# An attention kernel's turns: six score tiles set aside instead of five, P.V sums copied by ScalarE

## The chip, the cores and the metric

The kernel runs on one core of a Trainium2 chip. The metric is the device time of one execution in microseconds (us). All data are 32-bit floats; matmuls of linear layers and scores take operands of the type fp32r, and where more precision is needed an operand is split into a high and a low part and three products are added (high x high, high x low, low x high).

## What is computed

With x of 2048 rows by 512, 32 heads of 16, and a feed-forward part with 1792 hidden columns:

```python
q, k, v = split_heads(layernorm(x) @ wqkv)
p = softmax(einsum("bhqd,bhkd->bhqk", q, k) * 16 ** -0.5)
s = merge_heads(einsum("bhqk,bhkd->bhqd", p, v)) @ wo
h = relu(layernorm(x) @ w1 + b1) ** 2          # einsums in the reference
out = x + s * silu(h @ w2 + b2)
```

(In the reference the feed-forward part takes the same normed x.)

## The kernel before, in words

After a preparation of some 135 us (norms, transposes, q, k and v) comes the main part, the loop `for n in range(TURNS)` at the end of `fast_path`: 64 turns. A turn handles eight steps of attention; a step is one block of 128 keys against 512 queries for four heads. Two turns make up the 16 key blocks of one group of four heads (`qd`) and one chunk of 512 queries (`qc`). The order of instructions on every engine is written out by hand: no scheduler moves anything, and an instruction waits on semaphores for what it needs.

**Scores.** A step has two score pairs. A pair is two matmuls over 64 rows each (one in either half of TensorE's rows, side by side), which write the transposed scores of two heads, 128 keys by 2 x 512. A *direct* pair goes to one of two rotating PSUM buffers S of two banks each (`scores`), and ScalarE takes its exp from there into a tile P in SBUF (`exps`, line 519, form P<-S, 128x1024). A pair *set aside* (`aside`) goes half by half into two single banks, `sides[0]` = acc and `sides[1]` = lin; VectorE copies each half to the tile P (line 538), and ScalarE takes the exp later, from SBUF to SBUF (form P<-P).

**The linear work of a turn.** Beside the scores a turn runs a pair of blocks of the feed-forward layers or of the output projection (`Block`, `lin`), two outputs of 128x512, each of 12 products that are cut into two halves of 64 rows. Each block owns one bank of the tile `spare`. Half way, at the *row swap* (`swap`), the blocks change row halves; since two row halves may not write one bank at a time, GpSimd sets a one-element tile (`note`, line 588) when the products so far are done, and the first product after the swap waits for that: the fence.

**The row string.** The order of a turn on TensorE is a string. One letter is one *slot*, two matmuls over 64 rows side by side: S is a direct score pair, L a half of either block, B both halves of a pair set aside, 0 or 1 one half of such a pair (into acc or lin) beside one half of a block, / the swap, which is no slot. An ordinary turn's string has 40 slots, numbered 0 to 39 here:

```python
ORDINARY = "SLLSBLLLSLL0SL1LSLL/SBLLSLL0SL1LSLL0L1SLS"
```

TWO_PAIRS, SHORT and FIRST are the strings of turns 2, 16, 30 and 44, of turns 56 and 57, and of turn 0. Of a turn's 16 score pairs the first nine and the last two are direct, five are set aside. ScalarE's queue holds the exps in the order: the first nine, the five, the last two, which belong to the next turn's first step.

**P.V and what follows.** After its 40 slots a turn multiplies the P tiles of eight steps by V (`values_of`, line 866): 64 records of 128 rows by 32 columns, summed in the bank acc. Then `finish(n)`: after an even turn VectorE copies the sum to a tile `ou` (line 889), after an odd one it adds acc to that (line 892), and SP stores the result with five DMAs (`zd`, four `ud`), behind which the row sums are loaded again (`zc`, line 910), to be read by VectorE at the end of the next turn's slots (lines 903 to 915). At the start of each turn `see` (lines 1129 and 1130) lets ScalarE and VectorE touch the last tile set aside in the turn before.

VectorE and GpSimd also split weights and hidden values into parts (`split_piece`, `evict` in `first`): VectorE casts, GpSimd subtracts (line 120). `pieces_of` gives each turn 0, 1 or 2 such weight pieces; a second, late one falls to turns 6 and 10 of every 14. `middle` holds the turns (13, 14, 27, 28, 41, 42, 58, 59) with an extra tanh on ScalarE.

Of the kernel before, what the change touches and what calls it, by code (L numbers as in the profile page):

```python
# [28 lines left out]
OP = mybir.AluOpType  # L29
# [47 lines left out]
def fast_path(tc, sb, banks, env):  # L77
# [7 lines left out]
    dve, act, pool, sp = nc.vector, nc.scalar, nc.gpsimd, nc.sync  # L85
# [6 lines left out]
    def t(shape, dt, tag):  # L92

        cnt[0] += 1
        if tag in BUFS:
            turn[tag] = turn.get(tag, -1) + 1
            n = turn[tag] % BUFS[tag]
            p, tag = ps.get(tag), f"{tag}{places[n] if tag == 'S' else n}"
        else:
            p = None  # L100
        return (p or ps.get(tag, sb)).tile(shape, dt, tag=tag, name=f"{tag}_{cnt[0]}")
# [10 lines left out]
    def cast(eng, dst, src):  # L112
        if eng is act:
            act.copy(dst, src)
        else:
            eng.tensor_copy(dst, src)  # L116
# [392 lines left out]
    ptile = {}  # L509

    def score(i, p, hp, dst):
        qd, qc, kb = steps[i]
        k, q = ka[qd, kb // 8], qa[qd, qc]
        r = slice(64 * hp, 64 * hp + 64)
        mm(dst, k[r, p, 128 * (kb % 8):128 * (kb % 8) + 128], q[r, p], start=True, stop=True)  # L515

    def exps(i, p, src):
        if src is not None:
            act.activation(ptile[i, p], src, AF.Exp, scale=SCALE)  # L519

    def place(i, p):
        ptile[i, p] = t([128, 2, 512], FT, f"P{2 * ((i - 1) % 8) + p}")

    def scores(i, p):

        if i < len(steps):
            sc = t([128, 2, 512], FT, "S")
            place(i, p)
            for hp in range(2):
                score(i, p, hp, sc[:, hp])  # L530
            return sc

    def aside(i, p, hp):

        if hp == 0:
            place(i, p)
        score(i, p, hp, sides[hp])
        dve.tensor_copy(ptile[i, p][:, hp], sides[hp])  # L538
# [37 lines left out]
    def lin(*halves):  # L576
        done = False
        if pair[0]:
            for half in halves:
                j = half ^ swapped[0]  # L580
                done |= pair[0][j].issue(half, lin_banks[j])
        return done
# [11 lines left out]
    def end_pair():  # L594
        if pair[0]:
            while lin(0, 1):
                pass
            swapped[0], last, pair[0] = 0, pair[0], None
            last[0].evict()
# [46 lines left out]
    def second(c, g, i):  # L646
        ms = [m for m in range(len(PAIRS)) if PAIRS[m][0] == g]
        h, w = [hid[m] for m in ms], [wf[2, m] for m in ms]

        def evict():  # L650
            if g == 0:
                y[c, i] = t([128, 2, 512], FT, f"y{i}")
            old = b2b.unsqueeze(1).broadcast_to([128, 2, 512]) if g == 0 else y[c, i]
            dve.tensor_tensor(y[c, i], spare, old, op=OP.add)
            if g == 3:
                complete.add((c, i))

        return [Block(lambda p, k, j=j: h[k // 2][p][:, k % 2, 128 * j:128 * j + 128],
                      lambda p, k: w[k // 2][p][:, k % 2], range(2 * len(ms)), evict)
                for j in (2 * i, 2 * i + 1)]  # L660
# [8 lines left out]
    fill = []  # L669
    for c in ORDER:  # L670
        for m in range(len(PAIRS)):
            fill.append([lambda m=m: first(m)])
            if m in (1, 2, 4, 6):
                makes = [lambda c=c, g=m // 2, i=i: second(c, g, i) for i in range(2)]
# [188 lines left out]
    def values(i, first, last):  # L863
        qd, qc, kb = steps[i]
        for j in (1, 2, 3, 0) if i % 2 else (0, 1, 2, 3):
            mm(sides[0][32 * j:32 * j + 32], vq[qd][:, kb, 17 * j:17 * j + 32], ptile[i, j // 2][:, j % 2],  # L866
               start=first, stop=last)

    part, early = [None], [None]

    def values_of(steps_now):
        for i in steps_now:
            values(i, i == steps_now[0], i == steps_now[-1])

    def finish_early():
        early[0] = t([128, 512], FT, "ou")
        dve.tensor_copy(early[0], sides[0])

    def finish(n):

        if n == TURNS - 1:
            return
        if early[0]:
            part[0], early[0] = early[0], None
            dve.tensor_tensor(part[0], sides[0], part[0], op=OP.add)
            return
        ou = t([128, 512], FT, "ou")
        if n % 2 == 0:
            dve.tensor_copy(ou, sides[0])
            part[0] = ou  # L890
            return
        dve.tensor_tensor(ou, sides[0], part[0], op=OP.add)  # L892
        qd, qc, _ = steps[8 * n]
        sp.dma_start(zdram[qd][qc], ou[16::32])
        for j in range(4):
            sp.dma_start(udram[qd // 2][qc][0, qd % 2, :, j], ou[32 * j:32 * j + 16])
        events.setdefault(2 * n + 2, []).insert(0, (load_rowsums, (qd, qc)))
        events.setdefault(2 * n + 3, []).insert(0, (rowsums, (qd, qc)))
# [140 lines left out]
    middle = {}  # L1039
    TURNS, LAST = len(steps) // 8, 8 * (NQ - 1)  # L1040
# [8 lines left out]
    for j, c in enumerate(ORDER):  # L1049
        for i in range(2):  # L1050
            n = per * (j + 1) + i - 1 if j < 3 else LAST + 2 + i
# [41 lines left out]
    def happen(time):  # L1093
        for fn, a in events.pop(int(2 * time), ()):
            fn(*a)
# [6 lines left out]
    sides = [t([128, 512], FT, "acc"), t([128, 512], FT, "lin")]  # L1102
# [23 lines left out]
    def see(i):  # L1126

        last = ptile[i, 1][:1, 1, 511:]
        act.copy(seen[:, :1], last)
        dve.tensor_tensor(seen[:, 8:9], last, sides[1][:1, :1], op=OP.max)  # L1130
# [4 lines left out]
    ORDINARY = "SLLSBLLLSLL0SL1LSLL/SBLLSLL0SL1LSLL0L1SLS"  # L1135
    TWO_PAIRS = "SLSLBLLSL/SBLLSLL0S1LSEVLLSLLB/SSLL0L1S"

    SHORT = "SLLSBLLLS0S1LL0S1/S0LL1SL0SL1L0LSS1"

    FIRST = "SLLSLLBLSLL0SL1LSLL/SBLLSLL0SL1LSLL0L1SLS"  # L1140
    for n in range(TURNS):
        i = 8 * n
        happen(n)
        makes = fill[n][:]
        pair[0] = makes.pop(0)()
        if n:
            see(i - 1)
        pairs = [(k, p) for k in range(i + 1, i + 9) for p in range(2)]
        short = n in (LAST, LAST + 1)
        nd = 8 if short else 9  # L1150
        direct, asides = pairs[:nd] + pairs[14:], pairs[nd:14]
        later, aside_at = [], [0, 0]
        for row in TWO_PAIRS if makes else SHORT if short else ORDINARY if n else FIRST:
            if row == "S":
                k, p = direct.pop(0)
                sc = scores(k, p)
                if k == i + 8:
                    later.append((k, p, sc))
                else:
                    exps(k, p, sc)  # L1160
            elif row == "L":
                lin(0, 1)
            elif row in "01B":
                for hp in (0, 1) if row == "B" else (int(row),):
                    aside(*asides[aside_at[hp]], hp)
                    aside_at[hp] += 1
                if row != "B":
                    lin(1 - int(row))
            elif row == "/":
                swap()  # L1170
                if n == TURNS - 1:
                    make_last()
            elif row == "E":
                end_pair()
                pair[0] = makes.pop(0)()
            else:
                values_of(range(i, i + 2))
                finish_early()
        for j, (k, p) in enumerate(asides):
            exps(k, p, ptile[k, p])  # L1180
            if j == 0:
                for fn, a in middle.pop(n, ()):
                    fn(*a)
        for a in later:
            exps(*a)
        if n == TURNS - 1:
            two = t([128, 2, 512], FT, "S")
            for m in range(2):
                rest(m, two[:, m])
            rest(3, sides[1])  # L1190
        pieces_now = pieces_of[n] if n < len(pieces_of) else 0
        ahead = pieces_now > 0 and n % per in (0, 1, 3, 6, 7, 10, 11)
        while lin(0, 1):
            pass
        if ahead:
            split_piece()
        end_pair()
        if n == LAST + 4:
            gsb.update({(1, i): y[1, i] for i in range(2)})
        if n == TURNS - 1:  # L1200
            for m in range(2):
                end_rest(m, two[:, m])
            end_rest(3, sides[1])
        happen(n + 0.5)
        for _ in range(pieces_now - ahead):
            split_piece()
        values_of(range(i + 2 if early[0] else i, i + 8))
        finish(n)
    for time in sorted(events):
        happen(time / 2)  # L1210
# [7 lines left out]
    ou = t([128, 512], FT, "P0")  # L1218
# [158 lines left out]
```

## Time and profile before

| | |
|---|---|
| time, median of 3 runs (lowest to highest) | 1209.07 us (1208.68 to 1209.79) |
| profiled execution: its span, the only time of it that the page gives | 1207.8 us |
| what the median has above that span | 1.27 us |
| PE, DVE, ACT, POOL busy in the span | 1198.8, 843.3, 1042.3, 357.3 us |
| one ordinary turn (turn 24) | 533.50 to 549.97 us of the span |

The page names the engines PE (TensorE's matmuls), PEld (its weight loads), DVE (VectorE), ACT (ScalarE), POOL (GpSimd) and SP (SyncE, which issues most DMAs). L515 is line 515 of the kernel. A timeline row has the start, the time from the first start to the last end of the instructions merged in it, engine, line, operation, the names out<-in and the sizes, the number of instructions, and in brackets the idle time before them with what ended it. In matmul rows S<-QA,KA is a direct score pair, acc<-QA,KA or lin<-QA,KA a half set aside, S with other inputs a product of a block, and acc<-P,V is P.V. A group's row ends with busy time, mean ns of one, idle time before them and its releasers.

### The profile page before, as it was taken

The page shows a single profiled execution, that of the slowest core. Times are in us where ns is not written, and L with a number is a line of the kernel's source. Part 1 is how long each engine was busy: PE and PEld are TensorE (multiplying, and loading weights), DVE is VectorE, ACT ScalarE, POOL GpSimd, SP SyncE. Part 2 cuts the span into 40 slices and gives each one's busy share as a digit, 9 for nine tenths or more (in the row PEclk, how much of TensorE's full clock was granted, in tenths as well). Part 3 has the DMA queues.
Part 4 walks back from the last instruction along what each step waited for, and adds up shares of the span by engine and source line. Part 5 has one row for each costly group of instructions (what it writes and reads, how often), then busy time and mean ns, then how long its engine had stood idle before and what let it go on. Part 6 is the DMA issues. An engine that isn't in the chain of part 4 may idle for free.

```text
span 1207.8 us, 24222 instructions
## 1 busy us (share of the span) xinstructions
PE 1198.8 (99%) x9867; PEld 706.4 (58%) x9867; DVE 843.3 (70%) x1362; ACT 1042.3 (86%) x1232; POOL 357.3 (30%) x276
## 2 busy tenths in 40 slices
PE   9999999999999999999999999999999999999997
PEld 7888655555555555555555555555555555555554
DVE  6666767575867766757677666677775758777766
ACT  6655689889999899889999999889899889899984
POOL 5756523040312321304032122220230403322224
PEclk9999999999999999999999999999999999999999
DMA  7798914131353222224323223151422233455534
GB/s 291 292 377 319 333 58 137 45 110 45 97 154 108 72 67 84 72 79 149 119 77 100 60 88 95 45 169 43 133 80 80 78 100 80 132 188 172 160 109 141
DMA packets 107640, 155.17 MB, mean 128 GB/s; under 512 B 43386, under 2 KB 57736, under 8 KB 107524
## 3 DMA queue, kind: packets, MB, share of 16 engines
q1 hardware_dynamic: 104596, 144.60, 37.3%
q0 software_dynamic: 2352, 7.93, 2.1%
q8 instruction: 78, 1.28, 0.4%
q10 hardware_dynamic: 576, 1.05, 0.2%
q14 instruction: 38, 0.31, 0.1%
HBM read 103.87 MB, written 49.67 MB: 127 GB/s over the span
## 4 chain that ended last, share of the span: by engine, by line
PE 99%; DVE 0%; issue 0%; POOL 0%; ACT 0%; POOLq 0%; DVEq 0%
PE acc L866 37%; PE S L563 29%; PE S L515 15%; PE B L326 5%; PE acc L515 5%; PE B L127 4%; PE lin L515 2%; PE D L326 1%; PE D L253 1%; PE B L689 1%; PE S L1017 0%; PE lin L326 0%; PE acc L326 0%; DVE P L1261 0%; DVE P L1262 0%; PE S L326 0%
## 5 line engine op out<-in xcount | busy, mean ns | idle before, releaser
L519 ACT ACTIVATE P<-S 128x1024 f32<-128x1024 f32 x702 | 662.4, 1042 | 92.3 <-PE S L515 90.4
L866 PE MATMUL acc<-P,V 128*32 128x512 f32 x4096 | 453.5, 594 | 0.0
L538 DVE COPY P<-acc 128x512 f32<-128x512 f32 x322 | 222.7, 692 | 140.8 <-PE lin L515 67.9
L519 ACT ACTIVATE P<-P 128x1024 f32<-128x1024 f32 x322 | 315.4, 1092 | 0.0
L866 PEld LDWEIGHTS acc<-P,V 128*32 128x32 f32 x4096 | 126.2, 110 | 285.2 <-issue 265.6
L515 PE MATMUL S<-QA,KA 64*128 64x512 f32 x1404 | 290.4, 404 | 0.0
L538 DVE COPY P<-lin 128x512 f32<-128x512 f32 x322 | 220.5, 685 | 1.5 <-PE lin L515 0.6
L515 PEld LDWEIGHTS S<-QA,KA 64*128 64x128 f32 x1404 | 133.7, 183 | 112.8 <-issue 41.8
L515 PE MATMUL lin<-QA,KA 64*128 64x512 f32 x322 | 126.7, 393 | 0.0
L515 PE MATMUL acc<-QA,KA 64*128 64x512 f32 x322 | 126.4, 392 | 0.0
L120 POOL TENSOR_TENSOR wf1l<-wr,wf1h 128x1024 fp32r<-128x1024 f32 x28 | 68.5, 2446 | 176.9 <-DVE wf1h L116 108.4
L588 POOL MEMSET note<- 1x1 f32 x68 | 6.1, 89 | 381.6 <-PE S L563 381.6
L120 POOL TENSOR_TENSOR hl<-T,hh 128x1024 fp32r<-128x1024 f32 x28 | 80.0, 2858 | 52.9 <-DVE hh L116 52.9
L563 PE MATMUL S<-xl,wf1h 64*128 64x512 f32 x464 | 95.5, 389 | 0.0
L120 POOL TENSOR_TENSOR wf2l<-wr,wf2h 128x1024 fp32r<-128x1024 f32 x28 | 67.3, 2402 | 90.5 <-DVE wf2h L116 90.5
L563 PE MATMUL S<-xh,wf1l 64*128 64x512 f32 x480 | 90.9, 388 | 0.0
L563 PE MATMUL S<-wf2l,hh 64*128 64x512 f32 x448 | 90.1, 389 | 0.0
L892 DVE TENSOR_TENSOR ou<-acc,ou 128x512 f32<-128x512 f32 x31 | 21.4, 692 | 96.6 <-PE acc L866 88.9
L563 PE MATMUL S<-wf2h,hl 64*128 64x512 f32 x448 | 82.6, 388 | 0.0
L563 PE MATMUL S<-xh,wf1h 64*128 64x512 f32 x480 | 77.5, 391 | 0.0
L563 PE MATMUL S<-wf2h,hh 64*128 64x512 f32 x448 | 71.8, 393 | 0.0
L515 PEld LDWEIGHTS acc<-QA,KA 64*128 64x128 f32 x322 | 59.3, 184 | 16.9 <-DVE P L538 2.1
(379 smaller groups left out, 1431.0 us busy)
## 6 DMA issues: line engine op xcount, KB each, us to landing
wr<-in_B_w_dram SPq DMA_DIRECT2D x56, 512.0 KB
QA<-qd SPq DMA_DIRECT2D x128, 128.0 KB
KA<-kd SPq DMA_DIRECT2D x64, 256.0 KB
u<-ud SPq DMA_DIRECT2D x15, 512.0 KB
kd<-P SPq DMA_DIRECT2D x11, 512.0 KB
V<-vd SPq DMA_DIRECT2D x8, 664.0 KB
qd<-P SPq DMA_DIRECT2D x9, 512.0 KB
vd<-P SPq DMA_DIRECT2D x16, 280.0 KB
```

The source lines that it names most:

```text
L120: leng.tensor_tensor(lo, src, hi.bitcast(FT), op=OP.subtract)
L127: mm(dst, lhs(a, k), rhs(b, k), start=n == 0, stop=n == len(todo) - 1)
L253: nc.tensor.transpose(halves[k // 2][:, k % 2, 128 * j:128 * j + 128], xnorm[c, i][:, j, 128 * k:128 * k + 128], ident)
L326: mm(dst, left[a][:, k], right[b][:, k], start=n == 0, stop=n == 5)
L515: mm(dst, k[r, p, 128 * (kb % 8):128 * (kb % 8) + 128], q[r, p], start=True, stop=True)
L519: act.activation(ptile[i, p], src, AF.Exp, scale=SCALE)
L538: dve.tensor_copy(ptile[i, p][:, hp], sides[hp])
L563: ins = mm(bank, self.lhs(a, k)[r], self.rhs(b, k)[r], start=n == 0 and self.at[other] == 0, stop=n == len(self.todo[half]) - 1 and self.a ...
L588: f = pool.memset(note[:, notes[0]:notes[0] + 1], 0.0)
L689: ins = mm(idle[:, :128], ident, ident, start=True, stop=True)
L866: mm(sides[0][32 * j:32 * j + 32], vq[qd][:, kb, 17 * j:17 * j + 32], ptile[i, j // 2][:, j % 2], start=first, stop=last)
L892: dve.tensor_tensor(ou, sides[0], part[0], op=OP.add)
```

## The change

45 of the 64 turns change (1, 3 to 12, 17 to 26, 31 to 40, 45 to 55, 61 to 63): those for which `six(n)` holds, that is neither the first, nor one with TWO_PAIRS or SHORT, nor one in or just behind `middle`. In them

- six of the 16 score pairs are set aside, eight and two are direct, in the order of a new string SIX, again of 40 slots. It has no B; the halves of a pair set aside come in separate slots, which alternate between lin and acc, and two S stand ahead of the swap instead of one S and one B behind it;
- `see` comes at the end of the turn before, ahead of that turn's `finish`, in place of at the start;
- the P.V sum of the turn before is copied out of acc by ScalarE (24 times the plain copy after an even turn, 21 times the copy after an odd turn), and after an odd turn GpSimd adds the earlier sum, both operands in SBUF. The stores then wait for GpSimd.

`place` is called by whichever half of a pair comes first, and `middle` is read without being emptied.

```diff
-        if hp == 0:
+        if (i, p) not in ptile:
             place(i, p)
...
+    def six(n):
+        return 0 < n < TURNS and n not in (LAST, LAST + 1) and len(fill[n]) == 1 and n not in middle and n - 1 not in middle
...
-            dve.tensor_copy(ou, sides[0])
+            cast(act if six(n + 1) else dve, ou, sides[0])
             part[0] = ou
             return
-        dve.tensor_tensor(ou, sides[0], part[0], op=OP.add)
+        if six(n + 1):
+            act.copy(ou, sides[0])
+            pool.tensor_tensor(ou, ou, part[0], op=OP.add)
+        else:
+            dve.tensor_tensor(ou, sides[0], part[0], op=OP.add)
...
+    SIX = "S1SL0LL1SL0LSLLL0L1SS/L0LL1LS0LLS1L0SLL1S"
...
-        if n:
+        if n and not six(n):
             see(i - 1)
...
-        nd = 8 if short else 9
+        nd = 8 if short or six(n) else 9
...
+        if six(n + 1):
+            see(i + 7)
         finish(n)
```

TensorE around the swap of turn 24, before. S with QA,KA is a direct pair, acc and lin are halves set aside, S_278 is the tile of the two blocks; xh_701,wf1l are the last products before the swap, xh_700,wf1h the first behind it:

```order
L563 MATMUL S_278_1650<-xh_701_3914,wf1l_1083_6026 128x512 x4
L515 MATMUL S_1128_6310<-QA_1081_6020,KA_948_5302 128x512 x2
L515 MATMUL acc_1651<-QA_1081_6020,KA_948_5302 128x512
L515 MATMUL lin_1652<-QA_1081_6020,KA_948_5302 128x512
L563 MATMUL S_278_1650<-xh_700_3913,wf1h_1082_6025 128x512 x4
L515 MATMUL S_1131_6324<-QA_1081_6020,KA_948_5302 128x512 x2
```

The same place after the change:

```order
L515 MATMUL lin_1652<-QA_1064_6045,KA_935_5323 128x512
L563 MATMUL S_278_1650<-xh_691_3928,wf1l_1066_6051 128x512
L515 MATMUL S_1109_6336<-QA_1064_6045,KA_935_5323 128x512 x2
L515 MATMUL S_1111_6341<-QA_1064_6045,KA_935_5323 128x512 x2
L563 MATMUL S_278_1650<-xh_690_3927,wf1h_1065_6050 128x512 x2
L515 MATMUL acc_1651<-QA_1064_6045,KA_935_5323 128x512
```

Between the last product before the swap and the first behind it stood a direct pair and a pair set aside; now two direct pairs stand there, and the last product shares its slot with a half set aside.

ScalarE where turn 23 (odd) passes into turn 24, before (P<-S is a direct exp, P<-P one of a tile set aside):

```order
L519 ACTIVATE P_1109_6180<-P_1109_6180 128x1024
L519 ACTIVATE P_1111_6190<-S_1110_6189 128x1024
L519 ACTIVATE P_1113_6196<-S_1112_6195 128x1024
L1129 COPY seen_1653<-P_1109_6180 1x1
L519 ACTIVATE P_1117_6251<-S_1116_6250 128x1024
L519 ACTIVATE P_1119_6260<-S_1118_6259 128x1024
```

The same place after the change:

```order
L519 ACTIVATE P_1091_6205<-P_1091_6205 128x1024
L519 ACTIVATE P_1093_6210<-S_1092_6209 128x1024
L519 ACTIVATE P_1095_6221<-S_1094_6220 128x1024
L1136 COPY seen_1653<-P_1091_6205 1x1
L896 COPY ou_1096_6267<-acc_1651 128x512
L519 ACTIVATE P_1099_6278<-S_1098_6277 128x1024
L519 ACTIVATE P_1102_6287<-S_1101_6286 128x1024
```

The copy of acc, which needs turn 23's last P.V product, now stands ahead of turn 24's first exp.

VectorE from the end of turn 23's work to the first copies of turn 24, before:

```order
L654 TENSOR_TENSOR y_871_4874<-S_278_1650,y_871_4874 128x1024
L892 TENSOR_TENSOR ou_1114_6239<-acc_1651,ou_1085_6063 128x512
L1130 TENSOR_TENSOR seen_1653<-P_1109_6180,lin_1652 1x1
L538 COPY P_1120_6264<-acc_1651 128x512
L538 COPY P_1120_6264<-lin_1652 128x512
L538 COPY P_1123_6284<-acc_1651 128x512
L538 COPY P_1123_6284<-lin_1652 128x512
```

The same place after the change:

```order
L654 TENSOR_TENSOR y_860_4890<-S_278_1650,y_860_4890 128x1024
L1137 TENSOR_TENSOR seen_1653<-P_1091_6205,lin_1652 1x1
L538 COPY P_1100_6282<-lin_1652 128x512
L538 COPY P_1100_6282<-acc_1651 128x512
L538 COPY P_1103_6300<-lin_1652 128x512
L538 COPY P_1103_6300<-acc_1651 128x512
L538 COPY P_1108_6327<-acc_1651 128x512
L538 COPY P_1108_6327<-lin_1652 128x512
```

The addition from acc is gone from VectorE's queue, and the copies of the halves begin with lin.

More of the change, by code (lines that the diff above doesn't have):

```diff
@@ L1149, in fast_path @@
         short = n in (LAST, LAST + 1)
-        nd = 8 if short else 9
+        nd = 8 if short or six(n) else 9
         direct, asides = pairs[:nd] + pairs[14:], pairs[nd:14]
         later, aside_at = [], [0, 0]
-        for row in TWO_PAIRS if makes else SHORT if short else ORDINARY if n else FIRST:
+        for row in TWO_PAIRS if makes else SHORT if short else SIX if six(n) else ORDINARY if n else FIRST:
             if row == "S":
@@ L1181, in fast_path @@
             if j == 0:
-                for fn, a in middle.pop(n, ()):
+                for fn, a in middle.get(n, ()):
                     fn(*a)
```

## The prediction

> **What bounds the kernel now.** I read the page first: its busy table and its chain.
>
> ```profile
> span 1207.8 us, 24222 instructions
> ...
> PE 1198.8 (99%) x9867; PEld 706.4 (58%) x9867; DVE 843.3 (70%) x1362; ACT 1042.3 (86%) x1232; POOL 357.3 (30%) x276
> ...
> PE 99%; DVE 0%; issue 0%; POOL 0%; ACT 0%; POOLq 0%; DVEq 0%
> ```
>
> TensorE (PE) carries the end, but ends of matmuls are modelled, so a busy share of 99% can still hide short waits. I therefore went to the table of stretches for one turn (turn 24; columns: length, then busy time of PE, PEld, DVE, ACT, POOL) and to TensorE's timeline of it.
>
> ```profile
> 533.50:549.97 16.47, 16.47 (x150) 9.18 (x146) 13.48 (x21) 14.95 (x17) 4.17 (x3) 1.00 0.17 43
> ```
>
> ```profile
> 533.50 0.50 PE L515 MATMUL S<-QA,KA 64*128 64x512 f32 x2
> 533.84 0.62 PE L563 MATMUL S<-xh,wf1h 64*128 64x512 f32 x4
> ...
> 535.68 0.85 PE L563 MATMUL S<-xl,wf1h 64*128 64x512 f32 x5
> ...
> 537.50 0.63 PE L563 MATMUL S<-xh,wf1l 64*128 64x512 f32 x4
> 537.96 0.44 PE L515 MATMUL S<-QA,KA 64*128 64x512 f32 x2
> 538.23 0.39 PE L515 MATMUL acc<-QA,KA 64*128 64x512 f32 x1
> ...
> 538.47 0.63 PE L563 MATMUL S<-xh,wf1h 64*128 64x512 f32 x4
> ...
> 539.62 0.39 PE L515 MATMUL acc<-QA,KA 64*128 64x512 f32 x1
> ...
> 542.63 0.40 PE L515 MATMUL S<-QA,KA 64*128 64x512 f32 x2
> 542.96 7.07 PE L866 MATMUL acc<-P,V 128*32 128x512 f32 x64
> 549.97 0.50 PE L515 MATMUL S<-QA,KA 64*128 64x512 f32 x2
> ```
>
> Starts count here, not lengths. P.V takes 549.97 - 542.96 = 7.01 us. Before it stand the 40 slots of the turn's row string: slot 0 takes 0.34, slots 1 to 18 take 537.96 - 533.84 = 4.12 (0.229 each), slot 19, the first after the swap, 0.27, slot 20 0.24, slots 21 to 38 542.63 - 538.47 = 4.16 (0.231 each), slot 39 0.33; together 9.46. The best stretch, slots 9 to 18 from 535.68, runs at 0.228. So no order of the same 40 slots could win more than 9.46 - (0.34 + 38 x 0.228 + 0.33) = 0.13 us a turn; the two end slots stand where matmuls over 64 rows change to P.V's over 128, which no string avoids.
>
> What spoils slots is in the timeline of the weight loads (PEld; in brackets the idle time before, and what ended it):
>
> ```profile
> 537.89 0.19 PEld L515 LDWEIGHTS S<-QA,KA 64*128 64x128 f32 x2 [0.19 <-ACT P L519]
> ...
> 538.35 0.31 PEld L563 LDWEIGHTS S<-xh,wf1h 64*128 64x128 f32 x4 [0.15 <-POOL note L588]
> 538.81 0.18 PEld L515 LDWEIGHTS S<-QA,KA 64*128 64x128 f32 x2 [0.15 <-ACT P L519]
> ...
> 539.40 0.18 PEld L515 LDWEIGHTS acc<-QA,KA 64*128 64x128 f32 x1
> ...
> 542.48 0.19 PEld L515 LDWEIGHTS S<-QA,KA 64*128 64x128 f32 x2
> ```
>
> Around the swap three loads come late: a score pair waits for ScalarE's exp to free its bank, the swapped linear matmul for GpSimd's fence, then another pair for ScalarE. A load 0.12 ahead of its matmul is early enough (538.35 to 538.47), so the second and third cost nothing at once; the first cost slot 19 its extra 0.04. But after such a run the slots stay at 0.231, while slots 9 to 18, with none late, settled at 0.228. I read the one as the cause of the other; the trace shows the order, no more.
>
> **The change part by part.** *TensorE.* 40 slots and 64 P.V records again: nothing added.
>
> *The swap.* The last linear pair before it starts one slot after 537.50, at 537.73; the first after it starts at 538.47, 0.74 later, its load 0.62 later.
>
> ```profile
> 538.21 0.09 POOL L588 MEMSET note<- 1x1 f32 x1 [16.38 <-PE S L563]
> ```
>
> That 0.62 is the matmul's end, this memset and the way back, so the fence lets the first swapped matmul start 0.62 + 0.12 = 0.74 after the last unswapped one. The new string also has two slots between them (S S for S B). If ScalarE no longer delays the first, three slots would take 3 x 0.229 = 0.69, and the fence holds the rest back: the exp's 0.04 is replaced by 0.05 of fence. Ends: -0.05 if the fence comes sooner, +0.02; I take 0.
>
> *The score pairs after it.* Exps follow each other on ScalarE as its timeline shows, and the groups give the length of one (and of a copy, for later):
>
> ```profile
> 534.04 8.39 ACT L519 ACTIVATE P<-S 128x1024 f32<-128x1024 f32 x9 [1.52 <-PE S L515]
> 542.26 4.88 ACT L519 ACTIVATE P<-P 128x1024 f32<-128x1024 f32 x5
> ```
>
> ```profile
> L519 ACT ACTIVATE P<-S 128x1024 f32<-128x1024 f32 x702 | 662.4, 1042 | 92.3 <-PE S L515 90.4
> ...
> L114 ACT COPY P<-B 128x512 f32<-128x512 f32 x14 | 8.1, 586 | 7.0 <-PE B L127 7.0
> ```
>
> One lasts 1.04, the next starts (8.39 - 1.04) / 8 = 0.92 later (0.95 for the five set aside). In the new string pairs stand at slots 0, 2, 8, 12, 19, 20, 27, 31, 35, 39; a pair needs the bank of the pair two before. Counted from the turn's start, slot 19 starts at 0.34 + 18 x 0.229 = 4.46, its exp 0.43 later (as VectorE's copy does, below) at 4.89, slot 20's at 5.81; slots 27, 31, 35, 39 start near 6.3, 7.3, 8.2, 9.1 and need banks whose exps end near 5.9, 6.9, 7.8, 8.7. With 0.05 to the load and 0.12 to the matmul, each has 0.2 or more to spare. So the late loads after the swap go, except the fence's. Slots 21 to 38 should then look like slots 1 to 18: 4.12 for 4.16, and slot 39, whose load at 542.48 was late as well, perhaps 0.01 less: -0.05 a turn. Ends: 0, and 17 x 0.003 + 0.02 = -0.07.
>
> *ScalarE.* One exp goes from PSUM to SBUF (+0.03) and a copy of 128x512 joins: 14.95 + 0.03 + 0.59 = 15.6 of 16.47, so it does not become the bound. The copy waits for P.V's end with next turn's exps behind it. If it starts where VectorE's did, 0.14 into the turn (533.64, below), the first exp starts at 0.73 at the latest, now 0.54. It then ends at 1.77; slot 8 (1.94) wants its load by 1.82, and gets it. The copy's pitch is likely under 0.5, as an exp's is 0.12 under its length, which leaves 0.1. Cost 0; without that cover, 0.1 a turn. At the turn's other end: slot 31's exp starts near 7.7, then 0.92 + 6 x 0.95 + 2 x 0.92 brings ScalarE to 16.2, before it must copy at 16.6.
>
> *VectorE.* Twelve bank copies for ten, P.V's copy or addition gone.
>
> ```profile
> 533.64 0.69 DVE L892 TENSOR_TENSOR ou<-acc,ou 128x512 f32<-128x512 f32 x1 [5.71 <-PE acc L866]
> ...
> 538.66 0.69 DVE L538 COPY P<-acc 128x512 f32<-128x512 f32 x1 [0.72 <-PE lin L515]
> 539.27 0.68 DVE L538 COPY P<-lin 128x512 f32<-128x512 f32 x1
> ```
>
> A bank's round: matmul 538.23, copy 538.66, its end 539.35, next load 539.40, plus 0.12: 1.29, against 6 x 0.229 = 1.37. The new string spaces acc at slots 4, 10, 16, 22, 28, 34 and lin at 1, 7, 18, 25, 32, 38: six or more. Copies follow at 0.61 (538.66 to 539.27), alternation asks for one in three slots, 0.69. Only slots 18 and 34 come two slots after the other bank's; their copies start 0.15 late, but the next use of the bank is seven slots off or is P.V (about 0.1 left). Cost 0. What five slots cost stands in turn 56, where acc is used at 1062.69 and five slots on:
>
> ```profile
> 1062.69 0.39 PE L515 MATMUL acc<-QA,KA 64*128 64x512 f32 x1
> ...
> 1063.87 0.49 PE L515 MATMUL acc<-QA,KA 64*128 64x512 f32 x1
> ...
> 1064.20 0.49 PE L515 MATMUL S<-QA,KA 64*128 64x512 f32 x2
> ```
>
> That slot takes 0.33: 0.10 a miss.
>
> *GpSimd and the queues.* 21 turns get an addition of 128x512, priced by the group of that size; below it are GpSimd's timeline in turn 25, VectorE's there, and SP's in turn 24.
>
> ```profile
> L120 POOL TENSOR_TENSOR P<-P,P 128x512 fp32r<-128x512 f32 x7 | 9.0, 1302 | 5.1 <-ACT P L114 5.1
> ```
>
> ```profile
> 551.66 2.40 POOL L120 TENSOR_TENSOR wf2l<-wr,wf2h 128x1024 fp32r<-128x1024 f32 x1
> 554.67 0.09 POOL L588 MEMSET note<- 1x1 f32 x1 [0.61 <-PE S L563]
> ```
>
> ```profile
> 552.03 0.68 DVE L538 COPY P<-lin 128x512 f32<-128x512 f32 x1
> ```
>
> ```profile
> 534.36 0.54 SPq L894 DMA_DIRECT2D zd<-ou  x1
> ...
> 536.87 0.36 SPq L910 DMA_DIRECT2D zc<-zd  x1
> ```
>
> The addition runs from about 0.8 to 2.1 of the turn, ahead of the fence, due at 538.21 - 533.50 = 4.7; the late splits (wf2l above, done 0.61 before its fence) follow even turns, which have no addition. So 0. Cover gone, a late memset would cost its lateness, in 21 turns. The five stores on SP's queue (from 534.36) and, behind them, the load of the row sums (536.87) and whatever SP issues next move by 1.3; the sums are read after slot 39, past 542.96, four microseconds on: 0.
>
> VectorE's copies beside a GpSimd operation keep their length (0.68 at 552.03, with wf2l running to 554.06), so I add nothing for the new overlap. The Trainium skill (SBUF — State Buffer, Who interferes with whom) says that VectorE and GpSimd share a port pair as an exclusive lock, which a copy takes in its two-port modes; by that rule the addition would hold copies up, which is the rival D below. The trace bears out its exception for an instruction with at most one SBUF input.
>
> *Sum.* -0.05 x 45 = -2.25 us: the profiled span of 1207.8 becomes 1205.5. The shown runs' median, 1209.07, lies 1.27 above that span, so the forecast is 1206.8, its own range 1205.2 to 1208.4. About 0.2% (2.4 us) is what a measurement of this kernel can tell from no change: the forecast is at that edge.
>
> **The rivals.** *A: nothing gained.* If slots at 0.231 don't come from late loads, or if the alternating banks' loads, 0.02 to 0.04 late at six slots, unsettle them as well, the fence replaces the exp's wait and 1209.1 +- 1.5 stays. For it: a mean of 0.229 against 0.231 is little to build on. Against it: slots 9 to 18.
>
> *B: more.* If the fence comes early too, all 0.13 a turn go, 5.9 us: 1203.2. Against it: its 0.62 is the same chain in both orders.
>
> *C: slower, VectorE's banks.* The rounds have 0.08 to spare. If something (a second semaphore to wait for, two slots between the banks) makes a copy start over 0.08 later than I have it, each use misses by about 0.1 as in turn 56: one miss a turn gives 45 x 0.1 = 4.5, 1213.6; all of acc's five, 22, 1231. For it: margins thinner than any now in an ordinary turn. Against it: acc goes six slots now (538.23 to 539.62, its load at 539.40) without a wait.
>
> *D: slower, held copies.* If GpSimd's addition blocks copies, one held for 1.3 makes a score wait up to 1.2, in 21 turns: 25 us, 1234. Against it: 552.03. The same place holds the milder case, ScalarE's copy slower than 0.59: 0.1 x 45, 1213.6.
>
> **How the numbers follow.** Forecast 0.60, A 0.20, B 0.06, C 0.08, D 0.06. The forecast's range lies about half on each side of 1206.65, 0.2% below the median: faster 0.30 + 0.06 = 0.36, same 0.30 + 0.20 = 0.50, slower 0.14. The range leaves out B, C and D, 0.20: it reaches from 1204.9 to A's upper end and a little beyond, 1211.0.
>
> **What would show it.** In a changed turn: slot 19 near 0.23 with no load ended by ScalarE, the fence's load late and slot 20 near 0.28, slots 21 to 38 near 4.12, period 16.42; ScalarE ending before P.V. Wrong would be: loads at slots 10, 16, 22, 28, 34 ended by VectorE (C), late loads at slots 2 or 8 ended by ScalarE, copies over 0.75 beside the addition (D), or slots after the swap still at 0.231 with no load late (A).

## The result, and the profile after

| | before | after |
|---|---|---|
| time, median of 17 runs each (lowest to highest) | 1209.19 us (1208.42 to 1209.83) | 1211.36 us (1210.78 to 1211.98) |
| ratio, 95% interval | | 1.0019 (1.0012 to 1.0025) |
| span of the profiled execution | 1207.8 us | 1209.1 us |

The change costs 2.2 us. The forecast was 1206.8, its range 1204.9 to 1211.0: the result lies 0.36 above it, on the other side of no change. The page of the changed kernel (span, busy row, chain of the end):

```profile
span 1209.1 us, 24425 instructions
...
PE 1200.2 (99%) x9867; PEld 718.2 (59%) x9867; DVE 884.0 (73%) x1411; ACT 1072.9 (89%) x1273; POOL 384.0 (32%) x297
...
PE 98%; DVE 1%; DMA 0%; issue 0%; ACT 0%; DVEq 0%
```

TensorE still carries the end, with the same 9867 matmuls. VectorE, ScalarE and GpSimd have the work that was added and none has become the bound. (ScalarE copies 41 sums, not 45: behind the turns 2, 16, 30 and 44, which have TWO_PAIRS, VectorE still adds the sum, so the changed turns 3, 17, 31 and 45 have no copy on ScalarE.) So most of the loss is to be looked for inside TensorE's stream. One changed turn shows it (turn 20, the start of which is at 467.84; columns of the first fence as in the prediction: length, then PE, PEld, DVE, ACT, POOL):

```profile
467.84:484.32 16.48, 16.48 (x148) 9.60 (x145) 14.26 (x22) 15.67 (x18) 5.21 (x4) 1.00 0.17 43
```

TensorE's timeline of that turn, matmuls:

```profile
467.84 0.50 PE L515 MATMUL S<-QA,KA 64*128 64x512 f32 x2
468.18 0.39 PE L515 MATMUL lin<-QA,KA 64*128 64x512 f32 x1
...
470.03 0.62 PE L563 MATMUL S<-xl,wf1h 64*128 64x512 f32 x3
470.28 0.39 PE L515 MATMUL acc<-QA,KA 64*128 64x512 f32 x1
...
471.17 0.85 PE L563 MATMUL S<-xh,wf1l 64*128 64x512 f32 x5
471.65 0.39 PE L515 MATMUL acc<-QA,KA 64*128 64x512 f32 x1
...
472.33 0.62 PE L515 MATMUL S<-QA,KA 64*128 64x512 f32 x4
472.79 0.44 PE L563 MATMUL S<-xh,wf1h 64*128 64x512 f32 x2
473.06 0.39 PE L515 MATMUL acc<-QA,KA 64*128 64x512 f32 x1
...
476.99 0.40 PE L515 MATMUL S<-QA,KA 64*128 64x512 f32 x2
477.32 1.49 PE L866 MATMUL acc<-P,V 128*32 128x512 f32 x12
```

Slots 1 to 18 take 472.33 - 468.18 = 4.15 (before, in turn 24: 4.12), slots 19 and 20 0.46 together (0.27 + 0.24 before), slot 21 0.27, slots 22 to 38 3.93, slot 39 0.33. The exp's wait at the swap is gone and the fence's is there in its place, as forecast. But the turn is not shorter. Slots 9 to 13 run at (471.17 - 470.03) / 5 = 0.228; from slot 14 on, the next five take (472.33 - 471.17) / 5 = 0.232. The weight loads and VectorE's copies at that place:

```profile
470.07 0.18 PEld L515 LDWEIGHTS acc<-QA,KA 64*128 64x128 f32 x1
...
471.46 0.18 PEld L515 LDWEIGHTS acc<-QA,KA 64*128 64x128 f32 x1
...
472.10 0.42 PEld L515 LDWEIGHTS S<-QA,KA 64*128 64x128 f32 x4
472.73 0.19 PEld L563 LDWEIGHTS S<-xh,wf1h 64*128 64x128 f32 x2 [0.21 <-POOL note L588]
```

```profile
468.61 0.69 DVE L538 COPY P<-lin 128x512 f32<-128x512 f32 x1 [2.62 <-PE lin L515]
469.32 0.69 DVE L538 COPY P<-acc 128x512 f32<-128x512 f32 x1
...
470.71 0.69 DVE L538 COPY P<-acc 128x512 f32<-128x512 f32 x1
```

The load for acc at slot 16 (471.46) comes 0.06 after VectorE's copy of the use before has ended (470.71 + 0.69 = 471.40), and it had to wait for that: the matmuls of the slot before had already begun at 471.39, where most loads begin at once. It still comes 0.19 ahead of its own matmul (471.65), so it delays nothing that a row shows as a wait. Yet here the faster slots end. Before, in turn 24, acc was used at slots 4 and 11, seven slots apart. VectorE's copy of the first use and the load for the second:

```profile
534.96 0.69 DVE L538 COPY P<-acc 128x512 f32<-128x512 f32 x1 [0.57 <-PE lin L515]
```

```profile
535.92 0.18 PEld L515 LDWEIGHTS acc<-QA,KA 64*128 64x128 f32 x1
```

That copy had ended 0.27 ahead of the load, and the load came together with the matmuls of the slot before it. The changed kernel's swap itself (472.10) shows four loads of score pairs and no wait for ScalarE.

Such slots can be counted. For every changed turn ahead of the last (44 turns) I took the difference between the starts of consecutive slots, and the lateness of a load as its start less the start of the matmuls of the slot before. Slots fall in two groups: 0.225 to 0.228, mean 0.2267, called settled here, and the rest, mean 0.232. Means over the same 44 turns:

| us a turn | slot 0 | 1 to 18 | 19 to 21 | 22 to 38 | 39 | sum | settled, 1 to 18 | settled, 22 to 38 |
|---|---|---|---|---|---|---|---|---|
| before | 0.337 | 4.125 | 0.741 | 3.919 | 0.330 | 9.453 | 57% | 33% |
| after | 0.337 | 4.153 | 0.746 | 3.916 | 0.337 | 9.489 | 28% | 32% |

The sums differ by 0.037: 44 x 0.037 = 1.6 us. The last turn is 0.20 longer, the unchanged turns right behind changed ones 0.19 together, the other turns 0.05 shorter: +1.95 from the start of turn 1 to the end of the last turn. The rest of the measured 2.2 lies outside the span: a run of the changed kernel takes 2.04 us more than its own span in the mean, runs of the kernel before 1.77 to 1.80 (those beside the experiments, which list both). Of the experiments' kernels below, the three with the engine part have 2.02 to 2.05 and the others 1.77 to 1.79. So the engine part costs about 0.26 us that no row of a trace shows; why is open. (That the two spans differ by 1.3 only is the preparation and the tail, 0.6 shorter in this execution.)

The same counting tells what ends a settled run. I took the slots behind two settled ones, and the load that starts during such a slot, for the next one. Before (here over all its 54 turns with the ordinary string and 40 full slots), where that load was at most 10 ns later than the one before it, 481 of 482 slots were settled too; where it was later than that, 66 of 98 were. In the 44 changed turns the numbers are 153 of 178 and 32 of 74. So of the 67 ends there 42 come with a late load and 25 without one: the 10 ns are no sharp border. The late ones are halves set aside: median lateness 30, 24, 34, 20, 29 and 33 ns at slots 4, 10, 16, 28, 34 and 38, against 6 to 20 at the others from slot 2 on, but for slots 21 and 22 at the fence. That is rival A's mechanism, so far only read, not shown.

### The profile page after: what moved, and what is told of

Same layout as the page of the kernel before. It is cut to its first block, busy times and chain, and to the rows that moved or that the text cites. A ratio compares the mean times of both kernels' runs of the same rounds, so it can differ in the third digit from the quotient of the medians.

```text
span 1209.1 us, 24425 instructions
## 1 busy us (share of the span) xinstructions
PE 1200.2 (99%) x9867; PEld 718.2 (59%) x9867; DVE 884.0 (73%) x1411; ACT 1072.9 (89%) x1273; POOL 384.0 (32%) x297
## 4 chain that ended last, share of the span: by engine, by line
PE 98%; DVE 1%; DMA 0%; issue 0%; ACT 0%; DVEq 0%
PE acc L866 37%; PE S L563 29%; PE S L515 14%; PE acc L515 5%; PE B L326 5%; PE B L127 4%; PE lin L515 2%; PE D L326 1%; PE D L253 1%; PE S L1024 0%; PE lin L326 0%; PE acc L326 0%; DMA P<-in_A_x_dram 0%; DVE P L1272 0%; DVE P L1273 0%; PE S L326 0%
## 5 line engine op out<-in xcount | busy, mean ns | idle before, releaser
L519 ACT ACTIVATE P<-S 128x1024 f32<-128x1024 f32 x657 | 626.0, 1032 | 49.1 <-PE S L515 47.2
L519 ACT ACTIVATE P<-P 128x1024 f32<-128x1024 f32 x367 | 355.5, 1055 | 0.0
L538 DVE COPY P<-lin 128x512 f32<-128x512 f32 x367 | 252.6, 688 | 104.2 <-PE lin L515 99.1
L538 DVE COPY P<-acc 128x512 f32<-128x512 f32 x367 | 253.4, 690 | 77.5 <-PE acc L515 48.1
L515 PE MATMUL S<-QA,KA 64*128 64x512 f32 x1314 | 264.8, 404 | 0.0
L515 PE MATMUL lin<-QA,KA 64*128 64x512 f32 x367 | 144.2, 393 | 0.0
L515 PE MATMUL acc<-QA,KA 64*128 64x512 f32 x367 | 144.1, 393 | 0.0
L563 PE MATMUL S<-xh,wf1h 64*128 64x512 f32 x480 | 85.1, 395 | 0.0
L515 PEld LDWEIGHTS acc<-QA,KA 64*128 64x128 f32 x367 | 67.4, 184 | 19.3 <-DVE P L538 2.1
L515 PEld LDWEIGHTS lin<-QA,KA 64*128 64x128 f32 x367 | 67.5, 184 | 8.3 <-DVE P L538 0.9
```

The costliest lines, as they stand in the source:

```text
L563: ins = mm(bank, self.lhs(a, k)[r], self.rhs(b, k)[r], start=n == 0 and self.at[other] == 0, stop=n == len(self.todo[half]) - 1 and self.a ...
```

## The experiments

Theory J (near loads): the string's halves set aside reach their banks just as VectorE frees them, and each such load can end a settled run of slots. Rival E: what ScalarE and GpSimd now do costs the time. Rival M: the places of the letters cost it, whatever the banks do. Times are medians, and a kernel is compared with the runs of the kernel before in its own job.

| kernel | us | ratio to before, 95% interval | settled 1 to 18, 22 to 38 | slots 0 to 39, us |
|---|---|---|---|---|
| e1, engine part alone | 1212.93 | 1.0032 (1.0020 to 1.0044) | 40%, 32% | 9.533 |
| e2, string alone | 1210.73 | 1.0013 (1.0004 to 1.0022) | 24%, 28% | 9.489 |
| e3, one near load | 1209.91 | 1.0005 (0.9995 to 1.0014) | 44%, 38% | 9.467 |
| e4, even pairs | 1207.99 | 0.9991 (0.9982 to 1.0000) | 61%, 74% | 9.440 |
| e5, changed, short copies | 1206.29 | 0.9978 (0.9968 to 0.9987) | 54%, 76% | 9.406 |
| e6, before, short copies | 1208.38 | 0.9994 (0.9984 to 1.0003) | 68%, 41% | 9.442 |
| e7, even pairs, near loads | 1208.45 | 0.9995 (0.9986 to 1.0004) | 61%, 42% | 9.447 |
| e8, even pairs, engine part | 1211.07 | 1.0017 (1.0008 to 1.0026) | 42%, 67% | 9.496 |
| e9, even pairs, acc at slot 10 | 1208.41 | 0.9995 (0.9986 to 1.0004) | 45%, 78% | 9.442 |
| e10, the same, see early | 1207.39 | 0.9985 (0.9976 to 0.9994) | 45%, 79% | 9.426 |
| e11, acc at 11, see early | 1208.33 | 0.9994 (0.9985 to 1.0003) | 56%, 60% | 9.444 |

**The two parts of the change, each alone.** e1 is the changed kernel with the old string:

```diff
-        nd = 8 if short or six(n) else 9
+        nd = 8 if short else 9
...
-        for row in TWO_PAIRS if makes else SHORT if short else SIX if six(n) else ORDINARY if n else FIRST:
+        for row in TWO_PAIRS if makes else SHORT if short else ORDINARY if n else FIRST:
```

> The engine part of the change alone: ScalarE's copies, GpSimd's additions and the moved see stay, the 45 turns keep the row string ORDINARY with five pairs set aside. Theory J (late bank loads of the string): TensorE's slots are 0.2267 once they have settled and 0.232 until then; in the kernel before 56% of slots 1 to 18 and 33% of slots 22 to 38 are settled, in the changed one 27% and 32%, and the string does that, not the engines. J expects the shares of before (56% or a little more, since the load at slot 4 no longer waits for VectorE's sum; 33%) and 1209.2 +- 0.7 us. Rival E (ScalarE's copy or GpSimd's addition disturbs the turn): 1211.4, with the shares or the late loads of the changed kernel.

1212.93: neither theory has that number. In the trace slots 19 to 21 take 0.795 (0.741 before), and slots 1 to 18 4.151 (4.125). ScalarE's timeline and the weight loads, turn 24, which starts at 534.33 here:

```profile
534.47 0.59 ACT L896 COPY ou<-acc 128x512 f32<-128x512 f32 x1 [1.13 <-PE acc L866]
534.95 5.62 ACT L519 ACTIVATE P<-S 128x1024 f32<-128x1024 f32 x6
```

```profile
538.78 0.18 PEld L515 LDWEIGHTS S<-QA,KA 64*128 64x128 f32 x2 [0.27 <-ACT P L519]
538.89 0.19 PEld L515 LDWEIGHTS acc<-QA,KA 64*128 64x128 f32 x1
```

Behind the copy the first exp starts 0.62 into the turn (0.54 before). With the old string the pair at slot 19 waits for the chain of exps, its load now 0.234 late instead of 0.164 (medians), and pays for the shift. The four changed turns without a copy on ScalarE (3, 17, 31, 45) are the test of that: there the load at slot 19 is 0.160 late, and the slots together are 0.008 longer than before, against 0.104 in the other turns behind an even one and 0.072 behind an odd one. Turns behind an even one have no addition on GpSimd, so the copy is what costs. The engine part is not free by itself: it is free where no pair comes later for that chain.

e2 is the changed kernel with VectorE doing the sums:

```diff
-            cast(act if six(n + 1) else dve, ou, sides[0])
+            dve.tensor_copy(ou, sides[0])
...
-        if six(n + 1):
-            act.copy(ou, sides[0])
-            pool.tensor_tensor(ou, ou, part[0], op=OP.add)
-        else:
-            dve.tensor_tensor(ou, sides[0], part[0], op=OP.add)
+        dve.tensor_tensor(ou, sides[0], part[0], op=OP.add)
```

> The string alone: SIX in the 45 turns and see at the end of the turn before, but VectorE copies and adds P.V's sums as before; no copy on ScalarE, no addition on GpSimd. Theory J: 1211.4 +- 0.8 us, shares of settled slots near 27% (slots 1 to 18) and 32% (22 to 38), the load at slot 4 some 0.1 later than in the changed kernel. Rival E: 1209.2 +- 0.7.

1210.73, in J's range, with nearly the changed kernel's shares; its 44 turns are as long as those of the changed kernel, 9.489. So with this string the engines' part costs nothing in the changed turns. What it does cost stands in the unchanged turns 13, 27 and 41, behind changed ones: there VectorE's copy of the P.V sum starts 0.212 into the turn (0.144 before and in e2), behind a semaphore wait of its own of 21 ns that the trace has only here, and the load at slot 4, which waits for VectorE, is 0.204 late for 0.136. These three turns are 0.22 us longer together with the engine part and 0.06 without. For the changed turns E falls; what is left of it is these three turns and the 0.26 us outside the span. Rival D (held copies) falls with it: GpSimd's addition in turn 20 runs

```profile
468.71 1.30 POOL L897 TENSOR_TENSOR ou<-ou,ou 128x512 f32<-128x512 f32 x1 [12.50 <-ACT ou L896]
```

beside VectorE's copies from 468.61 and 469.32 above, which keep their 0.69. The Trainium skill (SBUF — State Buffer, Who interferes with whom) excepts VectorE instructions with at most one SBUF input, outside their two-port modes, from the shared ports' lock; these rows agree.

**Freeing the banks, TensorE's order untouched.** e5 changes what VectorE copies and nothing that TensorE issues (it leaves out half of the scores set aside, so it serves for the time alone); e6 is the kernel before with the same edit, the control:

```diff
+    def half_exps(i, p):
+        act.activation(ptile[i, p].rearrange("p h (r c) -> p h r c", r=2),
+                       ptile[i, p][:, :, 256:].unsqueeze(2).broadcast_to([128, 2, 2, 256]), AF.Exp, scale=SCALE)
...
-        dve.tensor_copy(ptile[i, p][:, hp], sides[hp])
+        dve.tensor_copy(ptile[i, p][:, hp, 256:], sides[hp][:, :256])
...
-            exps(k, p, ptile[k, p])
+            half_exps(k, p)
```

> The changed kernel, in which VectorE copies only 256 of the 512 columns of each half set aside, and ScalarE's exp of such a pair reads these 256 twice (the scores of the other 256 queries are left out and replaced by those); TensorE's order is that of the changed kernel, and every exp has its full size. A bank of a half set aside comes free some 0.2 to 0.3 us sooner, so that no load of TensorE comes near. Theory J: the settled runs are no longer broken: share of settled slots 1 to 18 from 27% to 50% or more, 22 to 38 from 32% to 50% or more, 18 x 0.25 x 0.0055 + 17 x 0.25 x 0.0055 = 0.048 us a changed turn, 45 x 0.048 = 2.2: 1209.2 +- 0.8 us. Rival M (the places of the letters, whatever the banks do): 1211.4 and the shares of the changed kernel.

> The control to it: the kernel before with the same short copies and the same exps. Its halves set aside already find their banks free, so theory J expects 1209.1 +- 0.6 and shares near 56% and 33%. If short copies speed up TensorE for another reason (less traffic on PSUM), it gains here as much as the changed kernel does: 1207.

e5 takes 1206.29, 5.1 less than the changed kernel, 3.7 of it in the 44 turns; the rest, in other turns, the preparation and the tail, I did not trace slot by slot. The control takes 1208.38; its interval holds no change, but it lies 0.7 below before, just under J's range, and its shares rose to 68% and 41%. So short copies win a little in the kernel before as well, far from the 5.1. Turn 20 again, which starts at 466.35 here: VectorE's copy of acc, the load for acc at slot 16, and the matmuls:

```profile
469.17 0.43 DVE L542 COPY P<-acc 128x256 f32<-128x256 f32 x1 [0.25 <-PE acc L515]
```

```profile
469.88 0.18 PEld L515 LDWEIGHTS acc<-QA,KA 64*128 64x128 f32 x1
```

```profile
466.68 0.40 PE L567 MATMUL S<-xh,wf1h 64*128 64x512 f32 x1
...
470.79 0.63 PE L515 MATMUL S<-QA,KA 64*128 64x512 f32 x4
471.25 0.44 PE L567 MATMUL S<-xh,wf1h 64*128 64x512 f32 x2
471.52 0.39 PE L515 MATMUL acc<-QA,KA 64*128 64x512 f32 x1
...
475.40 0.39 PE L515 MATMUL S<-QA,KA 64*128 64x512 f32 x2
475.72 1.07 PE L870 MATMUL acc<-P,V 128*32 128x512 f32 x8
```

The copy ends 0.28 ahead of the load that needs it. Slots 1 to 18 take 470.79 - 466.68 = 4.11, slots 22 to 38 475.40 - 471.52 = 3.88. Over the 44 turns 752 of 754 slots behind two settled ones, with no load over 10 ns later, are settled, and the settled share after the swap goes from 32% to 76%. J's mechanism holds, and M falls: the letters stand where they stood. J's number does not hold: the gain is over twice what it expected (settled runs also last to the end of the turn, where slot 39 falls from 0.337 to 0.319).

**One near load put in, both ways.** e3 is the kernel before with one half moved by a slot; e4 is the kernel before with another string, and e7 is e4 with two near loads behind the swap:

```diff
-    ORDINARY = "SLLSBLLLSLL0SL1LSLL/SBLLSLL0SL1LSLL0L1SLS"
+    ORDINARY = "SLLSBLLLSL0LSL1LSLL/SBLLSLL0SL1LSLL0L1SLS"
```

> The kernel before with two letters exchanged in ORDINARY (57 turns): the half into acc stands at slot 10, six slots after slot 4, in place of slot 11; nothing else. Theory J: its load comes 0.01 or more later than its neighbours and breaks the settled run in about 6 turns of 10, as such loads do in the changed kernel: slots 10 to 18, settled to 96% before, fall to about half, 9 x 0.45 x 0.0055 = 0.02 us a turn, 57 x 0.022 = 1.3, 1210.5 +- 0.7 us. Rival M (it is not the near loads but the string as a whole: more slots with one half of a score pair, other places of the S): slots 10 to 18 stay at 0.227, 1209.2 +- 0.5.

1209.91: the interval holds no change, so the time settles nothing. The slots do: settled 57% to 44% in slots 1 to 18, slot 10 from 77% to 18%, slots 14 on at 80% or more. The run recovers in some four slots, sooner than expected, and slots 1 to 18 lose 0.0125.

```diff
-    ORDINARY = "SLLSBLLLSLL0SL1LSLL/SBLLSLL0SL1LSLL0L1SLS"
+    ORDINARY = "SLLSBLLLSLL0S1LLSLLBS/LLLSL0LS1LLSL0LS1LS"
```

> Five pairs set aside and the engines as before, in the 57 ordinary turns another string: the direct pairs at slots 0, 3, 8, 12, 16, 20, 24, 28, 32, 36, 39, so that each finds its bank free with some 0.05 to 0.2 us to spare; B and S at slots 19 and 20 ahead of the swap; acc at 4, 11, 19, 26, 34, lin at 4, 13, 19, 29, 37 (one near load, lin at 19, right ahead of the fence). Theory J: without late loads after the swap slots 22 to 38 settle in some eight slots as slots 1 to 18 did before: share from 33% to 55 or 60%, 17 x 0.25 x 0.0055 = 0.023 us a turn and about 0.01 at slot 39, the exp's 0.045 at the swap against the fence's 0.05: 57 x 0.03 = 1.7, 1207.5 +- 0.9 us. Rival P (late loads of the score pairs are not what keeps the slots after the swap at 0.231; the row swap itself does): share stays at 33%, 1209.2 +- 0.7.

1207.99. Slots 22 to 38 settle to 74% (33% before), 3.875 instead of 3.919: the swap itself does not keep the slots behind it at 0.231, and P falls. That fits the premise of the prediction, late loads of score pairs, though e4 moves other letters too. But slot 39 now takes 0.386 (0.330), of which below.

```diff
-    ORDINARY = "SLLSBLLLSLL0S1LLSLLBS/LLLSL0LS1LLSL0LS1LS"
+    ORDINARY = "SLLSBLLLSLL0S1LLSLLBS/LLLS0LLS1L0SLLLS1LS"
```

> The string with even pairs (measured at 1207.99), after the swap of which slots 30 to 38 are settled in nearly every turn; here acc is used at slots 19, 25 and 31 in place of 19, 26 and 34, six slots apart, nothing else. Theory J: two near loads break the run, the share of slots 22 to 38 falls by 20 to 30 points, 17 x 0.25 x 0.0055 = 0.023 us a turn, 57 x 0.023 = 1.3: 1209.3 +- 0.8. Rival M: 1208.0 +- 0.5, the share unchanged.

Share 42%, slots 22 to 38 at 3.907, 0.032 a turn more than in e4; J had 0.023. The time rose by 0.46 only, inside both intervals and M's range, since slot 39 fell from 0.386 to 0.359: TensorE came later to a pair that had to wait anyway.

**The engine part where pairs have room.** e8 is e4's string with the engine part of the change in the 45 turns (edits as in e1 and e4).

> The string with even pairs and the engine part of the change in its 45 turns. The engine part alone cost 3.8 us with ORDINARY. Theory Q: ScalarE's copy puts off the first exp by 0.09 us and the whole chain of exps, and that costs time only where a score pair waits for the chain (slot 19 of ORDINARY, whose load was 0.23 late instead of 0.16). The even pairs have 0.05 to 0.2 to spare, so the engine part costs at most 0.5 us here, from near loads at slots 8 and 12: 1208.0 to 1208.7. Rival E (the copy on ScalarE, the addition on GpSimd or the later stores cost time by themselves): 1211 to 1212.

1211.07: Q's number fails by over 2 us, and E's range has it. I had overlooked that e4 has one pair that waits for the chain, the last. Its load and matmuls in turn 24, e4 and then e8:

```profile
541.94 0.19 PEld L515 LDWEIGHTS S<-QA,KA 64*128 64x128 f32 x2 [0.20 <-ACT P L519]
```

```profile
542.00 0.44 PE L515 MATMUL S<-QA,KA 64*128 64x512 f32 x2
542.37 1.06 PE L866 MATMUL acc<-P,V 128*32 128x512 f32 x8
```

```profile
542.81 0.19 PEld L515 LDWEIGHTS S<-QA,KA 64*128 64x128 f32 x2 [0.19 <-ACT P L519]
```

```profile
542.84 0.47 PE L515 MATMUL S<-QA,KA 64*128 64x512 f32 x2
543.24 1.07 PE L866 MATMUL acc<-P,V 128*32 128x512 f32 x8
```

Slot 39 takes 0.37 in e4 and 0.40 in e8 here, 0.386 and 0.418 over the turns (+0.032); slots 1 to 18 lose 0.020, with the loads of the score pairs at slots 8, 12 and 16 at 0.011 to 0.014 late, most others at 0.006. With the rest of the slots it is 0.056 a turn, 44 x 0.056 = 2.5 of the 3.1 us; some 0.26 more lies outside the span. The four turns without a copy on ScalarE lose nothing here either (-0.013 against e4; +0.087 and +0.040 in the others, behind even and odd turns). So Q's mechanism, the copy ahead of the chain of exps, stands with two places, not one, and it is not the whole cost.

**A faster version.** e9 and e11 change e4 in one respect each, e10 in both; the edits are the string

```diff
-    ORDINARY = "SLLSBLLLSLL0S1LLSLLBS/LLLSL0LS1LLSL0LS1LS"
+    ORDINARY = "SLLSBLLLSL0LS1LLSLLBS/LLLSL0LS1LLSL0LS1LS"
```

(e9 and e10) and

```diff
-        if n:
-            see(i - 1)
...
+        if n < TURNS - 1:
+            see(i + 7)
         finish(n)
```

(e10 and e11).

> The string with even pairs (1207.99) with the half into acc at slot 10 in place of 11 in all 57 turns. There VectorE copied acc of slot 11 just ahead of lin of slot 13, so that lin's load at slot 19 came 0.18 late and the two halves of the pair at slot 20 stood apart; the exps behind it ran 0.03 to 0.05 later, and the last pair, at slot 39, waited (0.386 for 0.33). With slot 10 lin is copied at once. Expected if that chain holds: the load at slot 19 some 0.03 late, slot 39 0.35 to 0.36, slots 1 to 18 worse by the 0.0125 that one near load cost: -0.015 to -0.02 us a turn, 1207.0 +- 0.7. If slot 39 waits for the chain of exps from slot 0 on, whatever happens at 19: 1208.5, the near load alone.

> The same, and see in every turn at the end of the turn before, ahead of the P.V sum, as the changed kernel has it in its turns (VectorE still copies and adds P.V's sums). Expected from the string alone: the load at slot 4 late by 0.09 in place of 0.137, which breaks no settled run since none stands there: 0 to -0.5 us against the run before it. If see on ScalarE comes to delay the last exps, slot 4 or P.V waits and the time rises by 0.05 a turn, 3 us.

> The string with even pairs with acc at slot 11 again and see at the end of the turn before in all turns. Expected from the parts: slots 1 to 18 at 4.122 as in the string with slot 11, in place of 4.136 with the near load of slot 10, the rest as in the run with see early: 57 x 0.014 = 0.8 less, 1206.6 +- 0.7 us. If slot 39 takes the gain back (TensorE comes sooner to a pair that waits for its exp), 1207.4 stays.

e9: slot 39 fell to 0.367, not quite as far as expected, and slot 19's load to 0.040 late; slots 1 to 18 lost 0.014 and slots 19 to 21 0.009. The sum is that of e4 but for 0.002, and 1208.41 is no gain. e10, 1207.39, is 1.0 below e9 where 0 to 0.5 was expected; it is the one version that computes everything and is faster than before with an interval that excludes no change, by 1.7 us. e11 should have been faster still or as fast, and is neither: 1208.33, its slots 22 to 38 are settled to 60% only. Why see early helps with the one string and not with the other is open.

## Why the prediction was wrong, point by point

- **The swap: exp's 0.04 replaced by 0.05 of fence, net 0.** Right: slots 19 to 21 went from 0.741 to 0.746, and the fence's load is the late one.
- **Score pairs after the swap: the late loads go.** Right; none is ended by ScalarE there. **Slots 21 to 38 then look like slots 1 to 18, 4.12 for 4.16.** Wrong in the size: 3.919 to 3.916 for slots 22 to 38. Slot 39, -0.01 forecast, +0.007.
- **VectorE's banks: cost 0.** This is the step that failed. The prediction set a bank's round at 1.29, counting 0.12 from load to matmul, against 1.37 for six slots, and took the load as early enough. In the 45 changed turns the 225 uses of acc six slots behind another show medians of 0.428 from matmul to copy, 0.692 for the copy, 0.053 to the load: 1.173. A load that is not to disturb starts with the slot before its own, 0.227 ahead: 1.40 against six settled slots, 1.36. So there is no spare 0.08 but 0.04 too little. Nothing is missed (no slot from 1 to 18 or 22 to 38 is over 0.242 in the 44 turns, so rival C's price is nowhere paid), but settled runs end, in both halves: +0.028 in slots 1 to 18, and the 0.04 behind the swap that the gone score waits had won. e5, where the banks are free sooner, runs its 44 turns at 9.406, 0.047 under before, and 0.036 under the control, which had won 0.011 by the same edit; the prediction had said 0.05.
- **Rival A** named this mechanism (loads 0.02 to 0.04 late unsettle slots as well), at 0.20, with the price of nothing gained. It was the right story with too small a price: the loss reaches slots that had been settled before.
- **ScalarE's copy: cost 0, 0.1 a turn without cover.** Right for the slots of this string (e2), and e1 shows an uncovered price: 9.533 against 9.453, 0.08. The prediction had looked for it at slot 8; e1 pays it at slot 19 and in settled slots ahead of it.
- **GpSimd and SP's queue: 0.** Right in the changed turns, as e2 shows.
- **The sum.** It kept the time outside the span as it was, without a reason; the engine part added about 0.26 there. (That the 1.27 it adds is less than the 1.77 to 1.80 fits a profiled execution some 0.5 slower than the median one; that alone does no harm to the sum.) Its own range is narrower than the ends of its terms: -0.12 and +0.02 a turn give 1203.7 to 1210.0. The result lies above these too.
- **Not foreseen:** the last turn, +0.20. It has fewer products between its halves, so that lin comes again after five slots and its load waits for VectorE, which is at least a part of the 0.20:

```profile
1186.04 0.18 PEld L515 LDWEIGHTS lin<-QA,KA 64*128 64x128 f32 x1 [0.29 <-DVE P L538]
```

  and the 0.19 of the unchanged turns behind changed ones.

The reading of "0.12 ahead is early enough" was taken from one load whose cost at once was nothing. The same paragraph blamed late loads for slots at 0.231, and those of the banks were not put to that test: the load at 539.40, rival C's own case of acc after six slots, already came 0.016 behind the matmuls of the slot before.

## What to carry to other kernels

A buffer's round that just fits is not free on an engine that runs at its pace: a load that need not wait in any row can still end a faster, settled run of matmuls, so count the spare time of a round to the point where the load would start by itself, not to the point where the matmul would slip. Work moved to another engine costs where something waits for that engine's chain, and the place can lie far down the turn or in the next one; find every such waiter before pricing the cover. And where a wait stands late in a turn, gains and losses ahead of it can vanish in it (slot 39 in e7).

## What the runs showed of the hardware

- TensorE's pairs of 64-row matmuls (512 columns) have two paces, 0.2267 and a mean of 0.232 us, both with loads in time. The slower one goes from 0.224 to 0.236 and turns into the faster after some four to eight undisturbed slots; the faster mostly goes on as long as no load comes more than some 0.01 later than the last (481 of 482 slots before, 752 of 754 in e5, but 153 of 178 in the changed kernel). What in TensorE makes it so is not settled by these runs. The Trainium skill (TensorE: Matmul & The Clock Gate, Back-to-back issue gap) gives about 216 ns for an isolated matmul of 512 columns and says that the spacing in a real stream is set by loads and matmuls both. The pace here, 227, is that of two side by side, and the runs agree that the loads have a part in it (e5 against the changed kernel).
- Loads that all come equally late do no harm: in e4 those of slots 23 to 38 are 0.031 to 0.036 late in the median, and 95% or more of slots 31 to 38 are settled.
- A copy that waits for one thing more starts later than the wait's own length. ScalarE's copy of the P.V sum starts 0.144 into the turn after odd turns and 0.198 after even ones (medians in the changed kernel); 18 of these 20 have a semaphore wait of 17 ns of its own ahead of it, none of the former. With VectorE such a wait, of 21 ns, cost 0.07 (turns 13, 27 and 41, above). In e1 slots 1 to 18 lose 0.048 in the turns with the copy after an even turn, 0.010 in those after an odd one.
